# Queries of the second half of the tokens by Strassen's product, two tiles at a time, behind the keys and values

## The chip, the core and the metric

The kernel runs on one core of a Trainium2 chip. TensorE (PE) multiplies matrices into PSUM banks; VectorE (DVE), ScalarE (ACT) and GpSimd (POOL) work on what lies in PSUM and SBUF (POOL on SBUF alone here); SyncE (SP) and ACT issue the DMAs. The metric is the device time of one execution in microseconds (us), and the median of several executions where there are several.

## The reference: what is computed

The input x has 2048 tokens of 640 features. It is normalised per token (xn), and two branches work on xn:

```python
q, k, v = split(xn @ wqkv)                       # 32 heads of 20
phi(p) = concat(softmax(p @ w_phi), softmax(-p @ w_phi))   # 40 features a head, for q and for k
kv, z = phi_k^T v, sum of phi_k over the tokens  # per head
s = concat((phi_q kv) / (phi_q z + 1e-6)) @ wo   # linear attention
g = silu(gelu(xn @ w1 + b1) @ w2 + b2)           # feed-forward, 640 -> 1536 -> 640
out = x + s * g
```

All arrays are float32.

## The kernel before, in words

**Precision.** A float32 product is made of three passes (`PASSES`): each operand is rounded into a high part and the rest (`hi`, `lo`), and hi·hi, hi·lo and lo·hi are summed in PSUM. ACT makes the high part by a copy into a rounded type, DVE or POOL the rest by a subtraction.

**Folding.** The query and key weights are first multiplied by `w_phi` per head (`fold`, L166 to L173: 12 matmuls of 120 columns for each of five chunks of 128 input rows). `fold_w` (L176) rounds the result into one slab per chunk: `wk_s` and `wq_s`. The values' weights are `wv_s`.

**Stage 1, tiles of tokens.** 16 tiles of 128 tokens are taken in pairs: pair q holds tile 2q (even) and 2q+1 (odd); pairs 0 to 3 are the first half of the stage, 4 to 7 the second. `xp` (eight blocks of 128 rows, for four pairs) and the small slabs `b12` hold the rounded rows of a pair, `xd` (nine blocks) the rounded differences of blocks of the two tiles of a pair (`t_sums`, `t_split`, L274 to L282). Those differences exist for the feed-forward, which multiplies by Strassen's scheme in seven parts.

`project(t, ws)` (L321) multiplies one tile by one of the three weights: five chunks, three passes, two halves of 320 columns, so 30 matmuls of 128x320 into a slot of two PSUM banks (`bankA`, three slots in turn). Keys and queries then go through the features: `feat1` (L339) takes maximum, minimum, the difference to the maximum and `nr` = minimum - maximum on DVE, and the mirrored half on POOL (L351); `feat2` (L355) is one exponential on ACT. For keys, `key_fin` (L387) sums each head (DVE, L364), takes the reciprocal (L389) and scales on POOL (L369). `value` (L372) copies values out on ACT (L378). `query` (L381) stores the unnormalised exponentials to DRAM, from ACT's DMA queue. `kv_pair` (L404) adds two tiles to the running kv sum, 256 small matmuls into one bank of the `B` pool (two banks), which it keeps until `kv_rest` (L601) copies it out.

Tile t of the main loops (L517 and L546) does: keys of t, the preparation of a later pair of rows (statistics, mean subtraction L299 on POOL, product L304 on DVE, rounding L250 on ACT and L252 on DVE), values of t, features and scaling of the keys, and then queries: two at t = 6 to 9, one at t = 10 to 15, and two behind the loop. The folds of the query weights are spread over tiles 3, 4, 5 and 6.

**Stage 2, feed-forward and rest.** Twelve units (two halves of tokens by six groups of hidden columns): 54 matmuls of 128x512 in seven parts (`part`, L649 to L659), the activation, 60 matmuls back (`down`, L680 to L688). The weights of a group in Strassen's forms come from `w1_forms` (L411): sums on POOL (L414), rounding on ACT (L425) and POOL (L426). Then the normalised query features are transposed through DRAM, multiplied by kv (L790, L797) and by `wo` (L843).

**What sets the order.** All of stage 1 has its order written out by hand on every engine: each engine runs its instructions in the order of the program, and so does SP with its DMAs. A buffer is reused when its last reader is done; the pools matter here: `slabs` (23 of 5 KB per partition), `rows` (11), `bankA` (3 slots of two banks), `bankB` (2).

Of the kernel before, what the change touches and what calls it, by code (L numbers as in the profile page):

```python
# [8 lines left out]
F32 = mybir.dt.float32  # L9
# [6 lines left out]
P = 128  # L16
# [7 lines left out]
GF = 2  # L24
# [22 lines left out]
def hedgehog_gated_mlp_kernel(ctx: ExitStack, tc: tile.TileContext, x, xt_in, wqk, bd, wv, wo, w1, b1, w2, b2, out_t):  # L47
# [48 lines left out]
    xd_dram = dram.tile([P, 9, 2, CW], F32, name="xd_dram")  # L96
    w1_dram = dram.tile([NG, P, 2, 2048], F32, name="w1_dram")
    g_dram = dram.tile([KC, P, 2, CW], F32, name="g_dram")
    z_dram = dram.tile([1440], F32, name="z_dram")
    st_dram = dram.tile([NT // 2, 2, P, 2], F32, name="st_dram")  # L100

# [74 lines left out]
    def fold_w(tl, cs, name, dst):  # L176
# [6 lines left out]
            dst.append(sl)  # L183
        return mm, lo


    xts = {}
    last_feat, by_hand = [None], [True]
# [147 lines left out]
    def heads(ps):  # L336
        return ps[:, :, :HALF].rearrange("p a (h d) -> p a h d", d=DH)

    def feat1(ps):  # L339
# [3 lines left out]
        nc.vector.tensor_reduce(mx[:], p4, axis=AX.X, op=OP.max)  # L343
# [6 lines left out]
        last_feat[0] = nc.vector.tensor_tensor(nr[:], mn[:], mx[:], op=OP.subtract)  # L350
        nc.gpsimd.tensor_tensor(e5[:, :, :, 1, :], nr[:, :, :, None].to_broadcast([P, 2, 16, DH]),  # L351
                                e5[:, :, :, 0, :], op=OP.subtract)
        return e.rearrange("p a b -> p (a b)")

    def feat2(ef):  # L355
# [46 lines left out]
    vs, es, phis, xns, wk_s, wq_s = {}, {}, {}, {}, [], []  # L402

    def kv_pair(t):  # L404
        for u in (t, t + 1):
# [139 lines left out]
    queries = iter(range(NT))  # L545
    for t in range(6, NT):  # L546
        u = t + 4
        pk = project(t, wk_s)
        if u < NT:
            if u + 1 < NT:  # L550
                x_in(u + 1)
            if t > 6:
                pair_stats(u)
            if u % 2:
                load_xr(u // 2)
        if t in (6, 8):
            spill(t // 2 - 1)
        if t % 2 == 0 and 6 < t < NT - 2:
            pair_sub((t + 2) // 2)
        es[t] = feat1(pk)  # L560
        if t == 6:
            pair_stats(u)
            pair_sub(4)
            fold_w(wqT, range(4, KC), "wq", wq_s)
        if t % 2 == 0 and t < NT - 2:
            pair_mul((t + 2) // 2)
        if t == 12:
            w1r = load_w1(0)
        if t % 2 and t < NT - 2:
            t_sums((t + 1) // 2)  # L570
        vs[t] = value(t)
        feat2(es[t])
        phis[t] = key_fin(es.pop(t))
        if t % 2 == 0 and 6 < t < NT - 2:
            pair_plain((t + 2) // 2)
        if t % 2 and t < NT - 2:
            t_split((t + 1) // 2)
        if t == 6:
            query(next(queries))
            query(next(queries))  # L580
            pair_plain(4)
        if t == NT - 1:
            w1f = w1_forms(w1r)
            next(w1f)
            next(w1f)
        if t >= 7:
            query(next(queries))
        if t % 2 == 0:
            kv_pair(t - 2)
        if t == NT - 1:  # L590
            next(w1f)
        if 7 <= t < 10:
            query(next(queries))
    t = NT - 1
    w2r = [load_raw(w2[f * P:(f + 1) * P, :]) for f in range(GF)]
    pq = project(next(queries), wq_s)
    e_14 = feat1(pq)
    next(w1f)
    w1g = next(w1f)

    def kv_rest():  # L601
        kv_pair(NT - 2)
        kvr = const.tile([P, 424], F32, name="kvr")
        nc.scalar.activation(kvr[:, :320], kvp[0][:, :320], AF.Copy)
        nc.scalar.activation(kvr[:, 320:400], kvp[0][:, 240:320], AF.Copy)
        return kvr


    def kv_state(kvr):
        nc.gpsimd.memset(bdk[:, :, 60:], 0.0)  # L610
# [250 lines left out]
    def w2_raw(g):  # L861
        return [load_raw(w2[f * P:(f + 1) * P, :]) for f in range(g * GF, (g + 1) * GF)]

    kvr = kv_rest()
    e_last = feat1(project(next(queries), wq_s))
    startup.close()
    phase1.close()
    early_psum.close()
# [232 lines left out]
```

## Time and profile before

| | |
|---|---|
| runs shown | median 658.69 us (658.28 to 658.7, three) |
| profiled execution | 658.55 us, its span 656.8 us |
| granted clock of TensorE | 0.999 |
| instructions | 11378 |
| stage 1 on PE | 0.84 to 246.2 us of the span |
| feed-forward, first unit | from 246.23 us |

How to read it: the span runs from the first to the last instruction of the profiled execution. Rows of groups give the line, engine, operation, what it writes and reads, the shapes and the count, then busy us and mean ns of one, and the idle time before them with what ended it. Rows of the timeline and of the chain begin with the start and the length in us. L12 is line 12 of the kernel before. The ends of matmuls are modelled, so the distance between starts is the better measure for them.

### The profile page before, as it was taken

To read this page: it belongs to the slowest core of one execution; us is meant where nothing else is said; L and a number is where in the kernel's file an instruction comes from. 1 tells how busy PE (TensorE), PEld (TensorE's weight loads), DVE (VectorE), ACT (ScalarE), POOL (GpSimd) and SP (SyncE) were. 2 spreads that over 40 slices of the span, in tenths; PEclk is the share of its full clock that TensorE was granted. 3 is DMA by queue.
4 is the path that set the end of the run, shared out by engine and by line. 5 is a ranking of instruction groups with operands and counts; after the bars stand their busy time and mean duration, and the time that the engine had idled before them with its cause. 6 is when DMAs were issued, how large, how long until landed. Compare 5 with 4: busy or idle time off the path is not lost.

```text
span 656.8 us, 11378 instructions
## 1 busy us (share of the span) xinstructions
PE 651.7 (99%) x4438; PEld 567.1 (86%) x4438; DVE 472.9 (72%) x725; ACT 228.5 (35%) x320; POOL 381.3 (58%) x340
## 2 busy tenths in 40 slices
PE   9999999999999999999999999999999999999997
PEld 9999999999999998888888888888888886766866
DVE  5785865887878557678979968859889899853232
ACT  3523313423232227252352454752232424032130
POOL 2755354859577356958778876364462967343321
PEclk9999999999999999999999999999999999999999
DMA  9706052735261236436998899695769499999962
GB/s 350 275 1 173 7 158 91 248 82 156 51 219 51 102 94 254 135 126 234 246 250 305 198 410 327 100 335 215 153 225 231 95 268 206 307 215 252 283 222 81
DMA packets 159680, 126.97 MB, mean 193 GB/s; under 512 B 88978, under 2 KB 127122, under 8 KB 158730
## 3 DMA queue, kind: packets, MB, share of 16 engines
q1 hardware_dynamic: 156890, 114.64, 60.5%
q10 hardware_dynamic: 2736, 11.60, 4.7%
q8 instruction: 35, 0.57, 0.4%
q14 instruction: 19, 0.16, 0.1%
HBM read 81.12 MB, written 45.10 MB: 192 GB/s over the span
## 4 chain that ended last, share of the span: by engine, by line
PE 98%; DVE 1%; DMA 0%; SPq 0%; issue 0%; DVEq 0%
PE pA L330 32%; PE pB L688 24%; PE pB L659 22%; PE pB L843 11%; PE pA L171 2%; PE pB L790 2%; PE kv L398 2%; PE pA L462 1%; PE pB L797 1%; PE pA L316 1%; DVE y L697 0%; DMA phi_t<-eq 0%; DVE wolh L767 0%; DVE dn L364 0%; SPq L756 0%; DVE wol L768 0%
## 5 line engine op out<-in xcount | busy, mean ns | idle before, releaser
L688 PE MATMUL pB<-hs,w2s 128*128 128x512 f32 x720 | 165.8, 389 | 0.0
L688 PEld LDWEIGHTS pB<-hs,w2s 128*128 128x128 f32 x720 | 135.0, 188 | 28.8 <-DVE y L697 0.8
L659 PE MATMUL pB<-xp,w1s 128*128 128x512 f32 x324 | 81.4, 389 | 0.0
L659 PE MATMUL pB<-xd,w1s 128*128 128x512 f32 x324 | 79.3, 389 | 0.0
L356 ACT ACTIVATE e<-e 128x1280 f32<-128x1280 f32 x32 | 40.7, 1272 | 92.1 <-POOL e L351 91.7
L843 PE MATMUL pB<-oT,wo 128*128 128x512 f32 (+1 forms) x315 | 72.3, 381 | 0.0
L659 PEld LDWEIGHTS pB<-xp,w1s 128*128 128x128 f32 x324 | 60.7, 188 | 12.8 <-DVE pB L926 0.3
L659 PEld LDWEIGHTS pB<-xd,w1s 128*128 128x128 f32 x324 | 60.8, 188 | 12.6
L369 POOL TENSOR_TENSOR eq<-eq,rc 128x1280 f32<-128x1280 f32 x16 | 37.9, 2370 | 55.5 <-DVE rc L747 37.5
L843 PEld LDWEIGHTS pB<-oT,wo 128*128 128x128 f32 x315 | 57.2, 188 | 13.8 <-PE pB L790 2.5
L369 POOL TENSOR_TENSOR e<-e,rc 128x1280 f32<-128x1280 f32 x16 | 39.0, 2441 | 46.9 <-DVE rc L389 46.6
L697 DVE TENSOR_TENSOR y<-pB,y 128x512 f32<-128x512 f32 x100 | 63.1, 675 | 1.4 <-PE pB L688 1.4
L351 POOL TENSOR_TENSOR e<-nr,e 128x640 f32<-128x640 f32 x32 | 43.8, 1369 | 29.1 <-DVE nr L350 26.4
L330 PE MATMUL pA<-wv,xp 128*128 128x320 f32 x384 | 59.7, 310 | 0.0
L330 PE MATMUL pA<-wk,xp 128*128 128x320 f32 x384 | 59.7, 310 | 0.0
L664 ACT ACTIVATE pB<-pB,b1t 128x512 f32<-128x512 f32 x48 | 31.8, 662 | 78.7 <-DVE pB L926 29.3
L330 PE MATMUL pA<-wq,xp 128*128 128x320 f32 x384 | 58.8, 309 | 0.0
L330 PEld LDWEIGHTS pA<-wv,xp 128*128 128x128 f32 x384 | 57.0, 188 | 0.0
L330 PEld LDWEIGHTS pA<-wk,xp 128*128 128x128 f32 x384 | 56.9, 188 | 0.1
L330 PEld LDWEIGHTS pA<-wq,xp 128*128 128x128 f32 x384 | 56.9, 188 | 0.0
L734 POOL TENSOR_TENSOR ez<-eq,zrep 128x1280 f32<-128x1280 f32 x16 | 47.4, 2964 | 1.2 <-DVE y L695 1.2
L426 POOL TENSOR_TENSOR w1s<-raw,w1s 128x640 fp32r<-128x640 f32 (+1 forms) x18 | 26.3, 1462 | 30.0 <-ACT w1s L425 30.0
(137 smaller groups left out, 995.6 us busy)
## 6 DMA issues: line engine op xcount, KB each, us to landing
raw<-in_w_dram SPq DMA_DIRECT2D x42, 320.0 KB, 7.3
e_dram<-e ACTq DMA_DIRECT2D x16, 640.0 KB, 3.0
eq<-e_dram SPq DMA_DIRECT2D x16, 640.0 KB, 6.0
phi_t<-eq SPq DMA_DIRECT2D x64, 160.0 KB, 4.2
phT<-phi_t SPq DMA_DIRECT2D x20, 480.0 KB, 6.8
xres<-in_xt_dram SPq DMA_DIRECT2D x20, 256.0 KB, 4.6
xt<-in_x_dram SPq DMA_DIRECT2D x15, 320.0 KB, 5.3
out_dram<-xres SPq DMA_DIRECT2D x18, 256.0 KB, 8.5
```

The lines of the kernel that those rows point to most:

```text
L171: mm = nc.tensor.matmul(ps[:, hf, o:o + 120], tl[:120, c, i, :], foldb[:120, i, :120], start=True, stop=True)
L330: nc.tensor.matmul(ps[:, hf, :HALF], stat_x(q, o, k, a), ws[k][:, b, hf * HALF:(hf + 1) * HALF], start=n == 0, stop=n == 3 * KC - 1)
L351: nc.gpsimd.tensor_tensor(e5[:, :, :, 1, :], nr[:, :, :, None].to_broadcast([P, 2, 16, DH]), e5[:, :, :, 0, :], op=OP.subtract)
L356: nc.scalar.activation(ef, ef, AF.Exp)
L369: nc.gpsimd.tensor_tensor(e3, e3, rc[:, :, None].to_broadcast([P, 64, DH]), op=OP.mult)
L426: nc.gpsimd.tensor_tensor(sl[:, 1, :n], src, sl[:, 0, :n].bitcast(F32), op=OP.subtract)
L659: nc.tensor.matmul(bank[ch][:], tl[:, a, off + wo_:off + wo_ + P], mov(blk, b), start=new and n == 0, stop=n == len(mms) - 1, skip_group_c ...
L664: nc.scalar.activation(ps, ps, AF.Gelu_apprx_tanh, bias=b1t[:, f:f + 1])
L688: nc.tensor.matmul(ps[:], ws[i][:, b, d * P:(d + 1) * P], hs[o][i][:, a, :], start=i == n == 0, stop=(i, n) == (GF - 1, 2), skip_group_che ...
L697: nc.vector.tensor_tensor(y, ps[:], y, op=OP.add)
L734: nc.gpsimd.tensor_tensor(zv, ef, zf, op=OP.mult)
L843: nc.tensor.matmul(ps[:, mv], w, o[:, mv], start=n == 0, stop=n == 15, skip_group_check=True)
```

## The change

The second half's eight queries (pairs 4 to 7) leave the loop and come behind the last values, two tiles at a time, by the same seven parts that the feed-forward uses; the row blocks are the same (`xp`, `xd`), now as the stationary operand, and the weights are the halves and sums of the query weights.

- `fold_pair` (tiles 4 and 5) takes the place of four `fold_w` calls. Beside the rounded slabs it makes four sums of 128x320 from the two folded chunks, in two `sr` rows. `s_hi` rounds them on ACT, `s_lo` on POOL, and SP stores them to `s_dram`. At tile 15, `s_back` loads them into four slabs `wqs`.
- `query_pair` runs seven parts with 6, 6, 9, 9, 6, 9 and 9 matmuls of 128x320. X and W share the slot of the even tile, Z is in that of the odd tile, whose second bank DVE fills; Y and V take a bank of `B` each in turn. Copies of X and Y (ACT) and sums (POOL one, DVE four) stand between the parts.
- The statistics, x loads and splits (`t_split`) of later pairs are at other tiles; the first weight forms of the feed-forward, the exponential and scaling of tile 15 and the stores of the pairs are hooked between the parts; the POOL half of an odd tile's features comes in the next pair (`later`).
- The kv steps of tiles 12 to 15 and the copy of the kv bank come behind the first and the second pair.

The diff, cut to its core:

```diff
+    def fold_pair(i):
+        pa, pb = (fold(wqT, c)[0] for c in (i, 2 + i))
+        a, b = (row([P, D], F32, "sr") for _ in range(2))
+        for c, ps in ((i, pa), (2 + i, pb)):
+            wq_s[c] = slab(F32R, f"wq{c}")
+            s3 = wq_s[c][:].rearrange("p s (a b) -> p s a b", a=2)
+            nc.scalar.activation(s3[:, 0], ps[:, :, :HALF], AF.Copy)
+            nc.vector.tensor_tensor(s3[:, 1], ps[:, :, :HALF], s3[:, 0].bitcast(F32), op=OP.subtract)
+        dve = lambda d, x, y, op: nc.vector.tensor_tensor(d, x, y, op=op)
+        nc.scalar.activation(b[:, HALF:], pa[:, 1, :HALF], AF.Copy)
+        dve(a[:, HALF:], pa[:, 0, :HALF], b[:, HALF:], OP.subtract)
+        dve(b[:, HALF:], pb[:, 1, :HALF], b[:, HALF:], OP.add)
+        dve(a[:, :HALF], b[:, HALF:], pa[:, 0, :HALF], OP.subtract)
+        dve(b[:, :HALF], pb[:, 0, :HALF], a[:, :HALF], OP.subtract)
+        return [(i, a), (2 + i, b)]
...
+    def s_lo(parts):
+        for k, r, hi in parts:
+            nc.gpsimd.tensor_tensor(r[:].bitcast(F32R), r[:], hi[:].bitcast(F32), op=OP.subtract)
+            nc.sync.dma_start(s_dram[k][:, 0], hi[:].bitcast(F32))
+            nc.sync.dma_start(s_dram[k][:, 1], r[:])
...
@@ tiles 2 to 5
-        if t == 5:
-            fold_w(wqT, range(2, 3), "wq", wq_s)
...
+        if t >= 4:
+            if t == 5:
+                s_lo(s_hi(srs[0]))
+            srs.append(fold_pair(t - 4))
         feat2(es[t])
         if t == 4:
             pair_plain(3)
-        if t >= 3:
-            fold_w(wqT, range(t - 3 + (t > 4), t - 2 + (t > 4)), "wq", wq_s)
         phis[t] = key_fin(es.pop(t))
+        if t == 5:
+            s_lo(s_hi(srs[1]))
...
+    QPARTS = (("X", "A11", 0, None), ("Y", "S2", 10, None), ("X", "A12", 2, ("A1k", 4)), ("V", "S3", 12, ("A2k", 7)),
+              ("Z", "S1", 8, None), ("W", "A22", 14, ("A2k", 16)), ("Z", "S4", 5, ("A1k", 7)))
...
+    def query_pair(q, hooks, later):
+        even, odd = bankA(), None
+        bank, seen = {"X": even[:, 0, :HALF], "W": even[:, 1, :HALF]}, set()
+        r1 = row([P, 2, HALF], F32, "qx")
+        r2 = row([P, 2, HALF], F32, "qu")
+        for i, (ch, wn, xb, extra) in enumerate(QPARTS):
+            if ch in "YV":
+                bank[ch] = bankB("q" + ch)[:, :HALF]
+            if i == 4:
+                odd = bankA()
+                bank["Z"] = odd[:, 0, :HALF]
+            mms = [(wn, k, b, xb + k, a) for k in range(2) for a, b in PASSES]
+            if extra:
+                mms += [(extra[0], 0, b, extra[1], a) for a, b in PASSES]
+            for n, (w, k, b, blk, a) in enumerate(mms):
+                nc.tensor.matmul(bank[ch], q_x(blk, a, q), q_weight(w, k)[:, b], start=ch not in seen and n == 0,
+                                 stop=n == len(mms) - 1, skip_group_check=True)
+            seen.add(ch)
+            if i == 0:
+                nc.scalar.activation(r1[:, 0], bank["X"], AF.Copy)
+            elif i == 1:
+                nc.scalar.activation(r1[:, 1], bank["Y"], AF.Copy)
+                nc.gpsimd.tensor_tensor(r2[:, 0], r1[:, 0], r1[:, 1], op=OP.add)
+            elif i == 3:
+                nc.vector.tensor_tensor(r2[:, 1], r2[:, 0], bank["V"], op=OP.add)
+            elif i == 4:
+                nc.vector.tensor_tensor(odd[:, 1, :HALF], r2[:, 1], bank["Z"], op=OP.add)
+            elif i == 5:
+                nc.vector.tensor_tensor(bank["W"], r2[:, 1], bank["W"], op=OP.add)
+                ee = feat1(even)
+            elif i == 6:
+                nc.vector.tensor_tensor(bank["Z"], r2[:, 0], bank["Z"], op=OP.add)
+            if i in hooks:
+                hooks[i]()
+        return ee, feat1(odd, later)
...
@@ tiles 6 to 15
+    XIN = {6: (11, 12), 7: (13, 14), 8: (15,)}
+    STATS = {7: (11,), 8: (12, 13), 9: (14, 15)}
+    XR = {7: 5, 9: 6, 11: 7}
...
-        if t == 12:
+        if t == 13:
             w1r = load_w1(0)
-        if t % 2 and t < NT - 2:
+        if t in (7, 9, 11, 13):
             t_sums((t + 1) // 2)
+        if t == NT - 1:
+            s_back()
+        if t == NT - 1:
+            t_split(7)
         vs[t] = value(t)
...
+        if t in (7, 9):
+            t_split((t + 1) // 2)
+        if t == 12:
+            t_split(6)
...
-        if t >= 7:
-            query(next(queries))
-        if t % 2 == 0:
-            kv_pair(t - 2)
...
+        if t % 2 == 0 and t < NT - 2:
+            kv_pair(t - 2)
         if 7 <= t < 10:
             query(next(queries))
...
+    for q in range(4, 8):
+        if q == 7:
+            w2r = [load_raw(w2[f * P:(f + 1) * P, :]) for f in range(GF)]
+        ea, eb = query_pair(q, {1: lambda: early_rest(q, ea), 3: lambda: late_rest(q, eb), **({0: lambda: feat2(es[NT - 1])} if q == 4 else {})}, later)
+        if q == 4:
+            kv_pair(NT - 4)
+        if q == 5:
+            kv_pair(NT - 2)
+            kvr = kv_rest()
```

`early_rest` (behind part Y) and `late_rest` (behind V) issue, for the pair before, the POOL half of its odd tile, its exponentials and its stores, and one step of `w1_forms`; in the first pair `early_rest` scales tile 15's keys.

More of the change, by code (lines that the diff above doesn't have):

```diff
@@ L184, in fold_w, with s_hi @@
         return mm, lo
+    srs = []
+    def fold_pair(i):
[13 more added lines that the diff above has]
+        return [(i, a), (2 + i, b)]
+    def s_hi(pairs):
+        out = []
+        for k, r in pairs:
+            hi = row([P, D], F32R, "sh")
+            nc.scalar.activation(hi[:], r[:], AF.Copy)
+            out.append((k, r, hi))
+        return out
+    def s_lo(parts):
[3 more added lines that the diff above has]
+            nc.sync.dma_start(s_dram[k][:, 1], r[:])
     xts = {}
@@ new lines, in store_e, with kv_rest @@
+    def store_e(t, ef):
+        nc.scalar.dma_start(e_dram[_tok(t)], feat2(ef))
+    def kv_rest():
+        kvr = const.tile([P, 424], F32, name="kvr")
+        nc.scalar.activation(kvr[:, :320], kvp[0][:, :320], AF.Copy)
+        nc.scalar.activation(kvr[:, 320:400], kvp[0][:, 240:320], AF.Copy)
+        return kvr
+    wq_f = []
+    queries = iter(range(NT // 2))
+    XIN = {6: (11, 12), 7: (13, 14), 8: (15,)}
+    STATS = {7: (11,), 8: (12, 13), 9: (14, 15)}
+    XR = {7: 5, 9: 6, 11: 7}
@@ L576, in hedgehog_gated_mlp_kernel @@
[L576 to L577 removed]
+        if t in (6, 8, 10, 12):
+            pair_mul(q)
+        if t == 13:
+            w1r = load_w1(0)
+        if t in (7, 9, 11, 13):
+            t_sums((t + 1) // 2)
+        if t == NT - 1:
+            s_back()
+        if t == NT - 1:
+            t_split(7)
+        vs[t] = value(t)
+        if t < NT - 1:
+            feat2(es[t])
+            phis[t] = key_fin(es.pop(t))
+        if t in (8, 10, 12):
+            pair_plain(q)
```

95 lines of the change are left out of this document (50 added, 45 removed).

## The prediction

> **What bounds the kernel now.** First the page: busy shares, granted clock, and the chain that ended last.
>
> ```profile
> span 656.8 us, 11378 instructions
> PE 651.7 (99%) x4438; PEld 567.1 (86%) x4438; DVE 472.9 (72%) x725; ACT 228.5 (35%) x320; POOL 381.3 (58%) x340
> PEclk9999999999999999999999999999999999999999
> PE 98%; DVE 1%; DMA 0%; SPq 0%; issue 0%; DVEq 0%
> ```
>
> TensorE (PE) is busy for 651.7 of 656.8 us at full clock, and 98% of the chain is PE's own work. So the next question is whether PE ever waits: the view of waits for PE, then the window of the stage that the change rebuilds.
>
> ```profile
> PE pA L462 <- PEq L1091: 0.8, 1, 0.8
> PE pB L797 <- DVE y L697: 0.4, 1, 0.4
> 158.00:246.00 88.00, 88.00 (x1073) 87.02 (x1072) 59.36 (x76) 25.82 (x30) 54.00 (x50) 1.00 0.34 107
> ```
>
> Two waits, 1.2 us in all, none in the projections. The window's columns are length, then PE, PEld, DVE, ACT and POOL: from 158 to 246 us PE has no gap, DVE is busy for 59 us and POOL for 54. So each matmul taken out here is worth its spacing, as long as the engines that empty the banks keep up. The spacing stands in the chain in order of time:
>
> ```profile
> 53.00 1.33 PE pA L171 x12
> 54.33 8.80 PE pA L330 x60
> 63.13 1.33 PE pA L171 x12
> ...
> 272.29 12.24 PE pB L659 x54
> ```
>
> Sixty matmuls of 320 columns take 8.80 us, **146.7 ns** each; the 54 of 512 columns of a feed-forward unit take 12.24 us, 226.7 ns. The last row matters twice: those 54 are the same seven parts that the change gives the queries, six or nine matmuls in a row into one bank. The two spacings differ by 80.0 ns for 192 columns, 0.417 ns a column, and both leave 13.3 ns beside the columns. Going by parts costs no more per matmul than going by projections.
>
> **What leaves PE.** Two tiles of queries cost 2 x 30 = 60 matmuls. A pair by parts costs 6+6+9+9+6+9+9 = 54, all still 128x320: 54 x 146.7 ns = 7.92 us in place of 8.80. Four pairs save 24 x 146.7 ns = **3.52 us**. Five folds of 12 matmuls, keys, values, the first eight queries and eight kv steps keep their number and only move.
>
> **What is added beside PE.** The prices, by line and shape in the stage from 80 to 247 us, and single rows of the timeline:
>
> ```profile
> L350 DVE TENSOR_TENSOR nr<-mn,mx 128x32 f32<-128x32 f32 x25 | 14.5, 579 | 0.0
> L351 POOL TENSOR_TENSOR e<-nr,e 128x640 f32<-128x640 f32 x24 | 33.0, 1378 | 25.2 <-DVE nr L350 23.0 <-issue 1.9
> L356 ACT ACTIVATE e<-e 128x1280 f32<-128x1280 f32 x24 | 30.6, 1273 | 87.5 <-POOL e L351 87.1 <-ACT e L356 0.4
> L369 POOL TENSOR_TENSOR e<-e,rc 128x1280 f32<-128x1280 f32 x11 | 27.2, 2473 | 26.7 <-DVE rc L389 26.3
> L364 DVE TENSOR_REDUCE rc<-e 128x64 f32<-128x1280 f32 x11 | 16.3, 1484 | 23.4 <-ACT e L356 23.4
> L389 DVE RECIPROCAL rc<-rc 128x64 f32<-128x64 f32 x11 | 6.1, 553 | 0.4
> L282 POOL TENSOR_TENSOR xd<-tt,xd 128x1152 fp32r<-128x1152 f32 x4 | 10.8, 2692 | 0.0
> L414 POOL TENSOR_TENSOR st<-raw 128x256 f32<-128x256 f32 x2 | 1.5, 741 | 0.0
> L426 POOL TENSOR_TENSOR w1s<-raw,w1s 128x640 fp32r<-128x640 f32 x1 | 1.6, 1567 | 0.0
> ```
>
> ```profile
> 52.08 0.42 DVE L252 TENSOR_TENSOR b<-pA,b 128x256 fp32r<-128x256 f32 x1 [0.54 <-ACT xp L250]
> 52.42 0.55 DVE L252 TENSOR_TENSOR xp<-pA,xp 128x384 fp32r<-128x384 f32 x1
> 55.53 0.82 DVE L182 TENSOR_TENSOR wq<-pA,wq 128x640 fp32r<-128x640 f32 x1 [2.57 <-ACT wq L181]
> 66.10 1.49 DVE L304 TENSOR_TENSOR xr<-xr,bc 128x1280 f32<-128x1280 f32 x1 [3.56 <-POOL xr L299]
> 208.06 0.82 DVE L343 TENSOR_REDUCE mx<-pA 128x32 f32<-128x640 f32 x1 [0.38 <-PE pA L330]
> ...
> 210.26 2.62 DVE L350 TENSOR_TENSOR nr<-mn,mx 128x32 f32<-128x32 f32 x1
> ```
>
> *Folds (tiles 4 and 5).* Each `fold_pair` adds four DVE sums of 320 columns from PSUM: between the 0.42 us for 256 columns and the 0.55 for 384, so 0.48, about 0.40 from start to start. They hold two of the three bankA slots longer, and the next value takes the first of them. With one fold fewer before it, tile 4 starts at 53.0, its folds end at 64.5, and value 5 asks for the slot at 70.2. DVE's product ends near 66.3 (now 67.6, a fold later); two roundings and three sums behind it end near 69.0. In tile 5 the second fold asks at 75.9 for the slot of key 5, which DVE leaves near 75.1 (from 69.4: rounding 1.5, sums 1.5, reciprocal 0.5, features 2.2). **Cover about 1 us each time, cost nothing**; if DVE comes later, PE waits by the excess, once per tile. ACT's copies, POOL's four subtractions (1.57 us each) and the eight stores on SP stand ahead of x rows, statistics and feature halves that are wanted a tile later: nothing.
>
> *Keys and values alone (tiles 10 to 15).* The window of 88 us holds the eight queries that go to the pairs: 35.2 us of PE, 8 x 1.38 of POOL and 8 x 2.7 of DVE. What stays has 52.8 us of PE for at most 43 us of POOL and 38 of DVE: nothing, though any pair of x rows that comes late stops PE by what it is late.
>
> *Weights back.* Four loads of 640 KB on SP, ahead of the last value:
>
> ```profile
> e_dram<-e ACTq DMA_DIRECT2D x16, 640.0 KB, 3.0
> eq<-e_dram SPq DMA_DIRECT2D x16, 640.0 KB, 6.0
> ```
>
> Their slabs come free, at the latest, as the last key projection uses up its weights, every 0.88 us. From its start, S2 is wanted after 9.7 us and S1 after 13.2. At 6.0 us each, overlapping: nothing; one after the other at 3.0 to 6.0, up to about 2 us once.
>
> *The query pairs.* At 0.88 us for six matmuls and 1.32 for nine, X ends at 0.88, Y 1.76, A12 3.08, V 4.40, Z 5.28, W 6.60, Z again at 7.92. New waits stand in PE's only queue, and the whole rest stands behind them. How long an emptied bank takes:
>
> ```profile
> 246.91 0.41 ACT L604 ACTIVATE kvr<-kv 128x320 f32<-128x320 f32 x1
> 247.65 0.60 ACT L675 ACTIVATE x<-pB 128x512 f32<-128x512 f32 x1 [0.20 <-PE pB L659]
> ```
>
> A12 waits for X's copy: 0.20 to start and 0.41 to run, 0.61 of the 0.88 us that Y gives. V needs the one B bank that kv leaves, so Y's copy: 0.61 of 1.32. The last part waits for DVE's sum of Z: 0.20 + 0.48 of W's 1.32. All fit if the engine is free. Once it isn't: in the first pair ACT has the exponential of tile 15 (1.27 us) between the copies. X's copy ends at 1.49, the exponential at 2.77, Y's copy at 3.2, and V starts at 3.25, not 3.08: **+0.17 us**. POOL's sum there stands behind a split (2.69) and tile 15's second half, which leaves the last part some 0.6 us of room. For all other waits, 0 to 1.5 us, I take 0.2: the rows leave room nearly everywhere.
>
> *Moved besides.* The kv steps of the last four tiles now follow the first and second pair, and the two copies of the kv bank follow them on ACT, ahead of the third pair's X copy: kv ends 0.88 us before X does, which covers 0.41 and a short second copy. The stores of exponentials go out from ACT in the pairs: two copies, two exponentials and one rounding, near 4 us of 7.92. On SP the loads of w1 go a tile later and those of w2 stay ahead of the feed-forward by at least a pair: nothing. Tile 15's scaling on POOL (2.47) is wanted only after the second pair.
>
> DVE does per pair two feature groups (2.20 from the maximum's start to that of `nr`, and 0.51 for `nr`) and four sums: 2 x 2.71 + 4 x 0.40 = **7.0 of 7.92 us**. It ends the last pair some 4.5 us behind PE. The feed-forward begins on the slot freed longest ago and comes to the last one as its fifth bank: nothing. Its first weight forms now come ahead of it.
>
> **The sum.** 658.55 (the profiled execution, 1.75 above its span) - 3.52 + 0.17 + 0.2 = 655.4 us. The median of the runs shown, 658.69, lies 0.14 above that execution: **655.5 us**.
>
> **Rivals.** *Small waits eat half.* Copies and POOL's sums come late in every pair. At 0.4 us a pair, 655.5 + 1.6 = 657.1. For it: POOL has up to 29 us of work in these 34 us (second halves 8 x 1.38, sums near 4 x 0.9, forms 4 x 0.74 + at most 4 x 1.57, a scaling and a split 5.2). Against: most of it is wanted a pair later.
>
> *DVE becomes the bound, and the kernel slower.* `nr` can stand behind POOL:
>
> ```profile
> 210.15 2.69 POOL L282 TENSOR_TENSOR xd<-tt,xd 128x1152 fp32r<-128x1152 f32 x1
> ...
> L350 DVE TENSOR_TENSOR nr<-mn,mx x32: 172/265/2624, 21.5 to 248.5; 128x32 f32<-128x32 f32 x32
> ```
>
> The `nr` at 210.26 took 2.62 us and ended as POOL's split did; the shortest took 0.17. POOL is fuller in the pairs than it was beside the queries. If every `nr` waits out a whole rounding of 1.57 us, a pair takes 2 x (2.2 + 1.7) + 1.6 = 9.4 us of DVE, 1.5 over PE: 655.2 + 4 x 1.5 = 661.2; at 2.6 each, 668. It decides from a mean `nr` of 1.4 us, where a pair takes 8.8. Against: the median is 0.265, most of POOL's operations here last 0.7 to 1.6 us, and the added sums read one operand from PSUM. The Trainium skill (SBUF — State Buffer, "Who interferes with whom") says that a VectorE instruction with two SBUF inputs and a GpSimd one that reads SBUF take one shared port in turn, each for its whole length, and that one SBUF input does not contend. By that rule `nr` is the only feature step exposed and the four sums are not; the 2.62 us row agrees.
>
> *No saving per matmul.* Were a matmul by parts to take 163 ns, 54 would cost the old 8.80: 658.7. The feed-forward's 226.7 ns speak against it.
>
> **Chances.** Forecast 0.66 (654.9 to 656.3 by itself), small waits 0.14, DVE bound 0.13, no saving 0.07. About 0.2% (1.3 us) is what a measurement of this kernel can tell from no change, so faster means below 657.4: 0.66 + 0.10 = 0.76; same 0.04 + 0.05 = 0.09; slower 0.13 + 0.02 = 0.15. Forecast and small waits hold 0.80: from 654.6 (nothing waits, less run to run spread) to 658.2 (1.5 us of waits in pairs, 1 at the folds and weights).
>
> **What will show it.** 1440 matmuls of 128x320 become 1416. The pairs should take 7.92 us each on PE, with a wait near 0.17 us before V of the first; the view of waits for PE should list little else in pA and pB. DVE should be near 7 us busy per pair, with `nr` near 0.6 us. Wrong would be a PE idle over 0.5 us in every pair (small waits), DVE without idle from the second pair on (DVE bound), waits on pA at 70 or 76 us (folds), a wait on the load of S2 or S1, or a spacing other than 146.7 ns.

## The result and the profile after

The change takes 661.31 us (median of 5 runs, 660.64 to 661.65) against 658.69 for the kernel before (5 runs, 658.2 to 658.89): ratio **1.0041**, interval 1.0026 to 1.0055. It is slower by 2.6 us; the prediction was 655.5, and its range ended at 658.2. First the head of the page and the shares of the chain, the same rows that were shown of the kernel before:

```profile
span 659.6 us, 11407 instructions
PE 649.7 (99%) x4414; PEld 564.1 (86%) x4414; DVE 486.5 (74%) x749; ACT 235.0 (36%) x334; POOL 390.5 (59%) x348
PE 67%; DVE 8%; POOL 3%; ACT 1%; issue 1%; DMA 0%; DVEq 0%; POOLq 0%
```

PE has its 24 matmuls fewer (4414 records for 4438) and 2.0 us less to do, and still the span is 2.8 us longer. PE's share of busy time, 99%, tells nothing of it. The chain does: PE fell from 98 to 67%, because the way back from the end now leaves PE in stage 1: from 217.04 us, where V of the first pair starts, back to 158.75 us it runs through DVE, POOL and ACT without one matmul. The view of PE's waits says where (in all, times, longest):

```profile
PE pA L363 <- DVE nr L383: 2.1, 2, 1.8
PE qV L616 <- ACT qx L622: 1.6, 1, 1.6
PE kv L435 <- issue: 0.9, 1, 0.9
PE pA L499 <- PEq L1211: 0.8, 1, 0.8
PE pB L919 <- DVE y L819: 0.4, 1, 0.4
```

The last two (the sequencer's L1211 and the feed-forward's `y`) stood before as well. The first three are new, and the timeline of PE places them (start, length, and in brackets the wait):

```profile
128.47 0.83 PE L435 MATMUL kv<-e,v 128*32 128x40 f32 x67
130.19 1.47 PE L435 MATMUL kv<-e,v 128*32 128x40 f32 x61 [0.88 <-issue]
131.59 2.02 PE L363 MATMUL pA<-wq,b 128*128 128x320 f32 x12
...
140.88 1.99 PE L363 MATMUL pA<-wv,b 128*128 128x320 f32 x12 [0.23 <-DVE nr L383]
...
198.91 4.64 PE L363 MATMUL pA<-wv,xp 128*128 128x320 f32 x30 [1.83 <-DVE nr L383]
...
217.04 1.14 PE L616 MATMUL qV<-wqs,xd 128*128 128x320 f32 x6 [1.61 <-ACT qx L622]
...
231.51 1.40 PE L435 MATMUL kv<-e,v 128*32 128x40 f32 x128
232.84 1.43 PE L616 MATMUL pA<-wq,xp 128*128 128x320 f32 x6
234.10 1.04 PE L616 MATMUL qY<-wqs,xd 128*128 128x320 f32 x6
...
249.06 1.55 PE L781 MATMUL pB<-xp,w1s 128*128 128x512 f32 x6
```

Starts are the better measure. The kv step of tiles 6 and 7 takes 131.59 - 128.47 = 3.12 us where the one at 231.51 takes 1.33: 1.8 lost, of which the view calls 0.88 a wait. Value 9 comes 0.4 late, value 14 2.0 (196.91 was due, by 146.7 ns a matmul), V of the first pair 1.8 (due at 213.95 + 1.32), and X of the third pair takes 1.26 for 0.88: 0.4. That is 6.4 us. The feed-forward began at 246.06 before (start of its first row; the kernel before):

```profile
246.06 1.55 PE L659 MATMUL pB<-xp,w1s 128*128 128x512 f32 x6
```

It begins 3.0 us later now, and 3.0 + 3.52 saved = 6.5: the losses account for the result. Behind that point the two kernels run alike: 610.5 us of span are left for 610.7 before.

**Two places, one chain.** The two large waits, at value 14 and at V, lie on the same way back. For value 14, DVE's part of the timeline of the kernel after, then POOL's:

```profile
191.01 2.58 DVE L285 TENSOR_TENSOR b<-xr,b 128x256 fp32r<-128x256 f32 x1
193.52 3.05 DVE L285 TENSOR_TENSOR xp<-xr,xp 128x384 fp32r<-128x384 f32 x1
...
198.69 0.18 DVE L383 TENSOR_TENSOR nr<-mn,mx 128x32 f32<-128x32 f32 x1
```

```profile
190.56 2.75 POOL L406 TENSOR_TENSOR e<-e,rc 128x1280 f32<-128x1280 f32 x1 [3.44 <-DVE rc L426]
193.28 2.87 POOL L315 TENSOR_TENSOR xd<-tt,xd 128x1152 fp32r<-128x1152 f32 x1
...
214.09 1.28 POOL L384 TENSOR_TENSOR e<-nr,e 128x640 f32<-128x640 f32 x1 [0.19 <-DVE nr L383]
```

DVE's two roundings of 256 and 384 columns take 2.58 and 3.05 us; the prediction's rows for these shapes, with one operand in PSUM, have 0.42 and 0.55. Here both operands lie in SBUF, and each ends within 0.5 us of POOL's instruction beside it: DVE at 193.59 and 196.57, POOL at 190.56 + 2.75 = 193.31 and 193.28 + 2.87 = 196.15. The features of tile 13 start behind them (196.49), and value 14 waits for their bank. The Trainium skill (SBUF — State Buffer, "Who interferes with whom") says that a VectorE instruction with two SBUF inputs contends with a GpSimd one that reads SBUF; the trace agrees.

Only the second of the two is new. The same roundings in the kernel before:

```profile
195.24 2.58 DVE L252 TENSOR_TENSOR b<-xr,b 128x256 fp32r<-128x256 f32 x1
197.74 0.55 DVE L252 TENSOR_TENSOR xp<-xr,xp 128x384 fp32r<-128x384 f32 x1
```

There too the first stood beside POOL's scaling (194.79 to 197.54), but POOL then had nothing to do: pair 6 had been split in tile 11 (183.09). The change moved this split to tile 12, beside the second rounding, and that is 2.5 us more for DVE.

For V, the row of ACT that matters:

```profile
215.40 1.27 ACT L393 ACTIVATE e<-e 128x1280 f32<-128x1280 f32 x1 [1.69 <-POOL e L384]
216.57 0.42 ACT L622 ACTIVATE qx<-qY 128x320 f32<-128x320 f32 x1
```

The exponential of tile 15 stands ahead of Y's copy, as foreseen, but it starts at 215.40, when POOL's second half (214.09) is done, and not when X's copy is.

### The profile page after: what moved, and what is told of

Its sections match the earlier page's. It is cut to its first block, busy times and chain, and to the rows that moved or that the text cites. A ratio compares the mean times of both kernels' runs of the same rounds, so it can differ in the third digit from the quotient of the medians.

```text
span 659.6 us, 11407 instructions
## 1 busy us (share of the span) xinstructions
PE 649.7 (99%) x4414; PEld 564.1 (86%) x4414; DVE 486.5 (74%) x749; ACT 235.0 (36%) x334; POOL 390.5 (59%) x348
## 4 chain that ended last, share of the span: by engine, by line
PE 67%; DVE 8%; POOL 3%; ACT 1%; issue 1%; DMA 0%; DVEq 0%; POOLq 0%
PE pB L810 24%; PE pB L781 22%; PE pB L965 11%; PE pA L616 3%; PE pA L363 3%; PE pB L912 2%; POOL e L384 2%; DVE b L285 1%; DVE rc L401 1%; ACT e L393 1%; DVE xp L285 1%; DVE nr L383 1%; PE qV L616 1%; DVE mx L376 1%; DVE mn L377 1%
## 5 line engine op out<-in xcount | busy, mean ns | idle before, releaser
L401 DVE TENSOR_REDUCE rc<-e 128x64 f32<-128x1280 f32 x16 | 23.7, 1483 | 23.5 <-ACT e L393 23.5
L968 POOL TENSOR_TENSOR xres<-gt,xres 128x256 f32<-128x256 f32 x20 | 14.3, 736 | 35.7 <-DVE gt L967 35.7
```

The costliest lines, as they stand in the source:

```text
L401: nc.vector.tensor_reduce(ss[:], ef.rearrange("p (g d) -> p g d", d=DH), axis=AX.X, op=OP.add)
```

## The experiments

Theory A: the matmuls saved are really saved, and the loss is order: work of DVE, POOL and ACT stands too late in their queues, above all in tiles 10 to 15 and the first pair, where the query projections that gave these engines 4.4 us a tile are gone. Theory C: the gap in the kv step comes from the two big stores beside it, which hold up PE's instructions. The rivals stand in the expectations: a chain too long in whatever order, or parts whose copies and sums eat the saving. All the matmuls stay in every kernel unless an edit says so. Line numbers shift by some lines from kernel to kernel.

### One wait or one suspect at a time

*e1: tile 15's exponential behind Y's copy.*

```diff
-{1: ..., 3: ..., **({0: lambda: feat2(es[NT - 1])} if q == 4 else {})}
+{1: ..., 3: ...}      # feat2(es[NT - 1]) first in early_rest, hook 1
```

> The changed kernel, but tile 15's exponential stands behind the copy of Y instead of ahead of it. Theory A (the key features come late on DVE and POOL in tiles 8 to 15, and the first pair inherits it through that exponential): V's wait of 1.8 us in the first pair falls under 0.3 us, the time from 661.3 to about 659.6 us; the other waits stay. Rival B (the parts themselves wait, for the one B bank or for the weights loaded back): V still waits 1 us or more, 661 us.

Measured: 661.07 us (660.45 to 661.59), ratio 1.004 [1.0025, 1.0055]. V's wait is gone, and no time is won. Value 14 waits 1.83 us as before, and this time TensorE ran slower behind the wait; PE's row, and two windows (length, busy PE, PEld, DVE, ACT, POOL, then the granted clock, the share of the DMA engines and GB/s):

```profile
199.28 6.17 PE L363 MATMUL pA<-wv,xp 128*128 128x320 f32 x30 [1.83 <-DVE nr L383]
```

```profile
200.00:202.00 2.00, 2.00 (x12) 2.00 (x11) 0.01 (x1) 1.27 (x1) 2.00 (x4) 0.70 0.00 0
202.00:204.00 2.00, 2.00 (x9) 2.00 (x8) 1.97 (x3) 0.00 (x0) 1.92 (x6) 0.50 0.00 0
```

Thirty matmuls take 6.17 us for 4.64: 1.5 us of the 1.8 that V no longer lost. That is the profiled run (661.59 us, mean clock 0.996). The three others had 0.999 and 1.000, too high for such a drop, and took 660.45 to 661.11; what kept them from the 659.6 expected is not shown.

*e2: POOL's split of pair 6 at tile 14.*

```diff
-        if t == 12:
+        if t == 14:
             t_split(6)
```

> The changed kernel, but POOL's split of pair 6 stands at tile 14 instead of tile 12. Theory A, in its form with the shared port (DVE's last rounding of pair 7 took 3.05 us because POOL's split ran, and the features of tile 13 came late): that rounding takes 0.55 us, value 14 no longer waits (2.0 us now), 658.8 to 659.3 us. Rival D (DVE has too much to do there whatever POOL does): the wait of value 14 falls by less than 0.7 us, 660.7 us or more.

Measured: 662.62 us (662.24 to 664.1), 1.0068 [1.0051, 1.0085]. The rounding of 384 columns is back at 0.55 us while that of 256 keeps its 2.59, and the wait at value 14 is gone: its cause is shown. V then waits twice as long, to the same moment (217.15 for 217.04). DVE's row, then PE's:

```profile
194.02 0.55 DVE L285 TENSOR_TENSOR xp<-xr,xp 128x384 fp32r<-128x384 f32 x1
```

```profile
217.15 1.15 PE L616 MATMUL qV<-wqs,xd 128*128 128x320 f32 x6 [3.29 <-ACT qx L622]
```

PE came to the pair 1.6 us earlier and DVE to the `nr` of tile 15 2.0, but the exponential of tile 15 did not: POOL now did the moved split (211.56, 2.67 us) ahead of tile 15's second half (214.20). Behind the wait the granted clock fell to 0.54 and 0.61 from 218 to 222 us, and the feed-forward begins 1.4 us later than in the change (250.42).

*e3: projections in place of the parts, in the change's order.*

```diff
-        ea, eb = query_pair(q, ...
+        ea, eb = query_two(q, ...     # project(2 * q), feat1, project(2 * q + 1), feat1
```

> The changed kernel with everything in its place, but the eight queries behind the values go by ordinary projections, 60 matmuls per pair; the sums of weights are still made and loaded and nobody uses them. Theory A (the loss comes from the order, the gain of the parts is there): 24 matmuls more cost 3.5 us, V's wait of 1.8 is gone, so about 663.1 us, with the wait of value 14 still near 2 us. Rival B (the parts cost what they save): 661.3 us or less.

Measured: 663.12 us (662.4 to 664.26), 1.0073 [1.0058, 1.0088], value 14 waits 1.82. So going by parts was worth 1.8 us in the change as it stands, and the order, together with the sums of weights that nobody uses here, costs 4.7 (663.12 - 658.46, the kernel before beside it).

*e4: the stores of exponentials 2 and 3 at tile 4.*

```diff
-        nc.scalar.dma_start(e_dram[_tok(t)], ef)
+        # t in (2, 3): kept, and both issued behind the store of t == 4
```

> The changed kernel, but the two stores of the exponentials of tiles 2 and 3, which ran just ahead of the kv step of tiles 6 and 7, are issued some 18 us later. Theory C (in that kv step PE ran out of instructions, because their fetch stood behind those stores): the gap of some 1.8 us in the step goes, 659.5 us. Rival (the gap has to do with where the step lies in PE's program, or is chance): it stays at the same place, 661.3 us, or is absent in the other kernels of this call too.

Measured: 663.09 us (661.88 to 663.78), 1.0069 [1.0054, 1.0084]. PE's rows:

```profile
128.88 1.39 PE L442 MATMUL kv<-e,v 128*32 128x40 f32 x128
...
141.32 1.88 PE L363 MATMUL pA<-wv,b 128*128 128x320 f32 x7 [2.05 <-DVE e L380]
```

The stores are the cause: the kv step (128 matmuls in the trace, not the 256 of the description of the kernel) has no gap. Whether they held up instructions, the second half of theory C, is another question (last section). But no time is won, since value 9 now waits 2.05 us for DVE and starts at 141.32 for 140.88. In tiles 6 to 9 too DVE sets when PE goes on, and the gap only hid it. Behind the wait the clock fell (0.50 from 142 to 144 us): the value's 30 matmuls take 147.35 - 141.32 = 6.0 us for 4.4, which makes e4 slower than the change.

### Two moves, and the cause in tiles 6 to 9

*e5: e1 and e2 together.*

> The exponential of tile 15 stands behind the copy of Y, and POOL's split of pair 6 comes at tile 14 instead of 12: both moves at once, each of which alone left one of the two waits standing. If the wait at value 14 (1.83 us) and the one before V of the first pair (1.61 to 1.77 us) come from one late chain of DVE and POOL in tiles 10 to 15 that can be put off (theory A): both below 0.3 us, 3.6 us less than 661.3, so 657.7. If that chain is too long whatever its order (rival): one of the two places, or the last part of the first pair, still waits over 1 us, 659.5 or more.

Measured: 661.36 us (659.63 to 663.19), 1.0042 [1.0027, 1.0057]. Theory A's number failed: both waits are gone, but the last part of the first pair waits 2.82 us. PE's row, then DVE's:

```profile
219.96 1.38 PE L616 MATMUL pA<-wqs,xp 128*128 128x320 f32 x6 [2.82 <-DVE pA L627]
```

```profile
216.56 1.49 DVE L401 TENSOR_REDUCE rc<-e 128x64 f32<-128x1280 f32 x1 [5.18 <-ACT e L393]
...
219.41 0.50 DVE L627 TENSOR_TENSOR pA<-qu,pA 128x320 f32<-128x320 f32 x1
```

DVE sat idle 5.18 us for tile 15's exponential, with the key sums of tile 15 ahead of the sums of V and Z in its queue; POOL's sum of Y stood behind two splits. That is wrong order again, or a chain that is too long; this run can't tell the two apart.

*e6: e4, and the statistics of tiles 7 to 9 behind that tile's maxima. e7: e4, and the rounding and stores of the second pair of S sums behind tile 6's features.*

```diff
-        for u in STATS.get(t, ()):
-            pair_stats(u)
         ...
             pair_mul(q)
+        for u in STATS.get(t, ()):      # e6
+            pair_stats(u)
```

```diff
-        if t == 5:
-            s_lo(s_hi(srs[1]))
         ...
             fold_w(wqT, range(4, KC), "wq", wq_s)      # t == 6
+            s_lo(s_hi(srs[1]))                         # e7
```

> The stores of exponentials 2 and 3 leave at tile 4 (as in the run before, which took 663.1 us and had a wait of 2.05 us at value 9), and the statistics of tiles 7 to 9 stand behind that tile's maxima and products, so that DVE does them while it would wait for the exponential. If the two statistics in one tile are the main cause of DVE's lateness at value 9: its wait falls to 0.75 us or less, the drop of the clock behind it goes, and the time is 660 to 661.5. If the cause is the rounding of the S sums and the full pool of rows at tile 6 (rival): the wait stays at 1.3 us or more, 662 to 663.

> The stores of exponentials 2 and 3 leave at tile 4, and the rounding of the second pair of S sums, with its four stores, stands behind the features of tile 6 instead of at the end of tile 5. If the S sums and the full pool of rows make DVE late from tile 6 on: the wait at value 9 falls from 2.05 us to 0.3 or less, 660 to 661. If the two statistics in one tile are the cause (rival): the wait stays at 1 us or more, 662 to 663.

Measured: e6 663.21 us (662.74 to 664.06), 1.0072 [1.0057, 1.0087]; e7 668.08 (667.65 to 669.88), 1.015 [1.0135, 1.0165]. Value 9 waits 0.79 us in e6 and not at all in e7, so both causes count, the S sums more. DVE's product for pair 4, in the kernel before, the change and e7:

```profile
92.72 1.49 DVE L304 TENSOR_TENSOR xr<-xr,bc 128x1280 f32<-128x1280 f32 x1 [2.82 <-POOL xr L299]
```

```profile
94.92 1.49 DVE L337 TENSOR_TENSOR xr<-xr,bc 128x1280 f32<-128x1280 f32 x1 [4.95 <-POOL xr L332]
```

```profile
91.65 2.82 DVE L337 TENSOR_TENSOR xr<-xr,bc 128x1280 f32<-128x1280 f32 x1 [2.83 <-POOL xr L332]
```

The S sums held POOL, and pair 4's rows came 2.2 us later. Both totals missed: PE came earlier to the later tiles and waited longer there (a kv step 1.49 and 1.37 us for POOL's scaling, V 3.44 and 3.64 us), and e7 has a new wait ahead of the feed-forward:

```profile
254.55 2.93 PE L787 MATMUL pB<-xp,w1s 128*128 128x512 f32 x6 [4.41 <-DVE e L380]
```

Its releaser, DVE's last product at 253.69, belongs to the odd tile of pair 7, the last that DVE empties; the change has no such wait. The reading is that the edit turned the rotation of the three slots, so that the feed-forward's first bank is another one; no trace shows a bank's number, and e9 and e11 test it.

*e8: all five moves (e1, e2, e4, e6, e7).*

> All five moves at once: stores of exponentials 2 and 3 at tile 4, statistics behind the maxima, rounding of the second pair of S sums behind tile 6's features, the split of pair 6 at tile 14, the exponential of tile 15 behind the copy of Y. The matmuls are those of the change. If the loss is all order (theory A for tiles 10 to 15, theory C and DVE's lateness for tiles 6 to 9): no wait over 0.5 us in stage 1, the feed-forward starts near 243, and the time is 655 to 656.5, below the kernel before. If DVE and POOL have too much to do in these stages whatever the order (rival): waits of 1 us or more are left in pA or qV, 658 or more.

Measured: 661.23 us (660.57 to 662.16), 1.0043 [1.0028, 1.0057]: missed. From 84 to 213 us PE loses 0.2 us in all. Then the last part of the first pair waits 2.12 us, as in e5, with a clock of 0.50 behind it (219 to 221 us), and the feed-forward waits 1.68, on a bank of pair 7's even tile.

### The first pair

*e9: e8, with tile 15's key sums (DVE) and the split of pair 7 (ACT and POOL) behind the sum of Z, and a DVE memset of one column in tile 13 that turns the slots by one. e10: the first pair's moves on e5. e11: e9 without the memset. e12: e9 with projections.*

```diff
+        if t == 13:                                          # not in e10, e11
+            nc.vector.memset(bankA()[:, 0, :1], 0.0)
-        if t == NT - 1:
-            t_split(7)
         ...
+    def behind_z():                                          # hook 4 of the first pair
+        phis[NT - 1] = key_fin(es.pop(NT - 1))
+        t_split(7)
+        w1g.append(next(w1f))
```

> The run with all five moves (661.2 us) still lost time at two places: 2.12 us before the last part of the first pair, behind which the clock fell, and 1.68 us before the feed-forward, whose first bank was the one of pair 7's even tile. Here, on top of the five moves, the key sums of tile 15 on DVE and the split of pair 7 stand behind the sum of Z in the first pair, and one VectorE memset of one column in tile 13 turns the three slots of bankA by one, so that the feed-forward's first bank is one that is free early. If the loss is all order (theory A): no wait over 0.5 us in stage 1, the feed-forward starts near 243.5, 661.2 - 2.1 - 1.7 - about 1.2 for the clock = 655.4 to 656.6. If DVE and POOL have too much to do whatever the order (rival): a wait of 1 us or more appears in a later pair or earlier tile, 657.5 or more.

> The change with the moves of tiles 12 to 15 and the first pair alone: exponential of tile 15 behind the copy of Y, split of pair 6 at tile 14, key sums of tile 15 and split of pair 7 behind the sum of Z. Stores, statistics and S sums stand as in the change. If the wait of 2.82 us before the last part came from DVE's sums standing ahead of the two of V and Z: it is gone, with the drop of the clock behind it, and 661.4 - 2.8 - 1.2 to 1.5 = 657.0 to 657.5; the gap of about 1 us in the kv step of tiles 6 and 7 stays. If putting it off only moves the wait (rival): a wait of 1 us or more in the first or second pair, 659 or more.

> The first kernel of this job without the memset of one column: the feed-forward's first bank is again that of pair 7's even tile. If the bank sets the wait before the feed-forward: 1.5 to 2 us there, ended by DVE's nr of that tile, and that much more time, 657.1 to 658.5. If not (rival): no wait, the same time as the first kernel.

> The first kernel of this job with the last eight queries as projections (30 matmuls a tile) in the place of the parts, in the same order: it costs 24 matmuls more on TensorE. If the parts bring their 146.7 ns a matmul once nothing waits: 3.5 us more than the first kernel, about 659.5. If the parts' copies and sums take back a share (rival): 2.5 us or less more, or the first kernel shows waits that are gone here.

Measured: e9 661.93 us (661.26 to 662.9), 1.0055 [1.0043, 1.0068]; e10 662.73 (662.38 to 663.72), 1.0069 [1.0056, 1.0083]; e11 662.87 (661.65 to 664.73), 1.0072 [1.0056, 1.0087]; e12 660.3 (659.43 to 660.88), 1.0028 [1.0016, 1.004]. Here the rivals were right. The first pair of e9 has no wait; the second stops PE for 3.04 us. PE, DVE and POOL of e9:

```profile
228.76 1.97 PE L621 MATMUL pA<-wqs,xp 128*128 128x320 f32 x6 [3.04 <-DVE pA L632]
```

```profile
220.10 2.57 DVE L383 TENSOR_TENSOR nr<-mn,mx 128x32 f32<-128x32 f32 x1
...
227.62 0.49 DVE L630 TENSOR_TENSOR qu<-qu,qV 128x320 f32<-128x320 f32 x1 [2.04 <-POOL qu L628]
```

```profile
217.62 2.37 POOL L406 TENSOR_TENSOR e<-e,rc 128x1280 f32<-128x1280 f32 x1 [4.08 <-DVE rc L433]
219.94 2.68 POOL L315 TENSOR_TENSOR xd<-tt,xd 128x1152 fp32r<-128x1152 f32 x1
...
226.72 0.87 POOL L628 TENSOR_TENSOR qu<-qx 128x320 f32<-128x320 f32 x1
```

`nr` of 32 columns takes 2.57 us, to the end of POOL's split (222.62): the rival's mechanism, in one place. But it is not what stops PE, for DVE then sits idle 2.04 us until POOL's sum of Y is done (227.59). POOL had waited 4.08 us for DVE's reciprocal, with the scaling, the split, four sums and the sum of Y behind it in its queue. e10 has the same wait at the same place (3.5 us). The parts were then no gain: e12, with 24 matmuls more, is 1.6 us faster than e9. The memset of tile 13 cost 1.3 us itself (its slot is emptied by DVE, and key 14 waits for it). e11's wait ahead of the feed-forward (1.7 us on pair 7's even tile, none in e9) confirms that turning the slots decides it; its time does so only roughly.

### The splits early

*e13: e8, with both splits where POOL idles. e14: e13 with projections. e15: e13 without the moves of tiles 4 to 9 (e4, e6, e7). e16: e13 with tile 15's key sums behind the sum of Z.* In e13 the split of pair 6 stands ahead of tile 14's exponential; ACT's half of pair 7's comes at the end of tile 14, POOL's half behind tile 15's second half of features; one memset takes the first bank of the feed-forward, so that its first part gets another.

```diff
         vs[t] = value(t)
+        if t == 14:
+            t_split(6)
         if t < NT - 1:
             feat2(es[t])
         ...
         if t == 14:
-            t_split(6)
+            t_hi(7)
         ...
         if t == NT - 1:
-            t_split(7)
+            t_split(7, False)      # POOL's half alone
         ...
+        if unit == 0:
+            nc.vector.memset(bankB()[:, :1], 0.0)
```

> The five moves, and the splits early: the split of pair 6 stands ahead of tile 14's exponential, the ACT half of pair 7's split at the end of tile 14 and its POOL half behind tile 15's second half of features, so that GpSimd does both where it waited for DVE's reciprocals. One memset on DVE takes the feed-forward's first bank, so that its first part gets a bank that is free early. If the loss is all order (theory A): POOL ends tile 15's second half near 210.2 in place of 212.7, the exponential ends near 212.3, the sums of V and Z come 0.3 us late at most, no wait over 0.5 us in the pairs, the feed-forward starts near 243.6, and 661.2 - 2.1 - 1.7 - 1.3 + 0.3 = 656.4 (655.6 to 657). If the parts leave DVE and POOL no room (rival): a wait of 1 us or more in the first or second pair, 658.5 or more.

> The first kernel of this job with the last eight queries as projections (30 matmuls a tile) in place of the parts, in the same order: 24 matmuls more, but none of the parts' copies and sums. If the parts bring their 146.7 ns a matmul once the order is right (theory A): 3.5 us more than the first kernel, about 659.9. If the parts' copies and sums take it back (rival): the same time as the first kernel or less.

> The change with the moves of tiles 12 to 15 alone, as in the first kernel of this job: stores, statistics and S sums of tiles 4 to 9 stand as in the change, so the kv step of tiles 6 and 7 keeps its gap of about 1 us and value 9 its wait of up to 0.4 us. If most of the loss is in tiles 12 to 15 and the first pair (theory A): 1.0 to 1.5 us more than the first kernel, about 657.6. If both stages matter as much (rival): 2.5 us more or above, 659 or more.

> The first kernel of this job with DVE's key sums of tile 15 (1.49 + 0.55 us) behind the sums of V and Z instead of ahead of them. If these sums are all that holds the first pair (theory A): 0.3 us less than the first kernel, 656.1. If the second pair then meets DVE late, as it did once (3.04 us there, behind a nr that waited 2.57 us for a split; rival): 1 us or more above the first kernel.

Measured: **e13 656.68 us** (7 runs, 655.17 to 657.24), ratio **0.997** [0.996, 0.9981], faster than the kernel before (658.4 beside it) and 4.6 us faster than the change; e14 658.98 (657.82 to 659.84), 1.0008 [0.9998, 1.0017]; e15 658.24 (657.96 to 658.96), 0.9998 [0.9989, 1.0007]; e16 656.89 (655.93 to 657.35), 0.9974 [0.9964, 0.9985]. The profile of e13: head, PE's waits, its first row of the feed-forward, and POOL's rows:

```profile
span 653.5 us, 11405 instructions
PE 648.3 (99%) x4414; PEld 563.5 (86%) x4414; DVE 485.2 (74%) x750; ACT 235.4 (36%) x334; POOL 390.7 (60%) x348
```

```profile
PE pA L510 <- PEq L1226: 0.8, 1, 0.8
PE pB L932 <- DVE y L832: 0.4, 1, 0.4
```

```profile
242.95 1.55 PE L794 MATMUL pB<-xp,w1s 128*128 128x512 f32 x6
```

```profile
202.50 2.70 POOL L319 TENSOR_TENSOR xd<-tt,xd 128x1152 fp32r<-128x1152 f32 x1
...
208.54 1.28 POOL L388 TENSOR_TENSOR e<-nr,e 128x640 f32<-128x640 f32 x1 [0.19 <-DVE nr L387]
209.77 2.69 POOL L319 TENSOR_TENSOR xd<-tt,xd 128x1152 fp32r<-128x1152 f32 x1
```

POOL's second half for tile 15 starts at 208.54, 0.9 us after the first pair began (1.9 in the change), and only the two waits of the kernel before are left. DVE's key sums and the sums of V and Z still come a little late: the first pair's last part begins at 214.60 where 214.29 was due, and up to there the chain followed back has no matmul from 125 us on. So the other engines set the pace up to that point in e13 too; it costs only 0.3 us there. The busy times are those of the change (POOL 390.7 for 390.5, DVE 485.2 for 486.5): the same work, another order. The feed-forward starts 3.1 us ahead of the kernel before, of 3.52 saved.

e15 misses its 657.6 by 0.6, but it is clearly nearer to theory A: the moves of tiles 12 to 15 are worth 661.31 - 658.24 = 3.1 us, those of tiles 4 to 9 another 1.6. e14 says what the parts bring in a good order: 2.3 us by the medians (3.0 between the two profiled runs, 3.2 between their feed-forwards, 246.15 and 242.95), less than the 3.5 expected and not nothing. e16 decides nothing: 0.2 us from e13, inside its spread. Why single runs of e13 lie between 655.2 and 657.2, with no wait in the profiled one (655.32), stays open.

## Why the prediction was wrong

- **24 x 146.7 ns = 3.52 us: right.** The parts keep the spacing. PE's rows of the fourth pair, six matmuls in 0.88 us and nine in 1.32:

```profile
242.02 1.04 PE L616 MATMUL qY<-wqs,xd 128*128 128x320 f32 x6
242.90 1.48 PE L616 MATMUL pA<-wq,xp 128*128 128x320 f32 x9
244.22 1.04 PE L616 MATMUL qV<-wqs,xd 128*128 128x320 f32 x6
```

- **"Keys and values alone: nothing": the step that failed.** It set 52.8 us of PE against sums of 43 and 38 us of POOL and DVE. These engines do not work side by side: a key goes DVE, POOL, ACT, DVE, POOL, and each waits for the last. In the change this chain runs from 158.75 to 217.04 us without a matmul in it. Beside this the step took DVE's 38 us from the kernel before, where one of the two roundings was stretched by POOL (2.58 and 0.55 us); the split that the change moved stretched the other as well (3.05), 2.5 us more in one tile. Before, 4.4 us of query projection in each tile covered such lateness. The step named the mechanism ("any pair of x rows that comes late stops PE by what it is late") and gave it no price: 2.0 us at value 14, and the lateness that V then waits for.
- **"+0.17" for V of the first pair: the right wait, but it measured 1.8 us.** It was worked out as if tile 15's features were done when the pair began. The pair began at 212.19; POOL came to the second half of these features 1.9 us later and ACT to the exponential 3.2 us later, with the copy of Y behind it in ACT's queue.
- **Folds: right for the waits it looked for** (no wait on pA from 53 to 84 us), **wrong for what it called wanted "a tile later: nothing".** The S sums' rounding came ahead of pair 4's rows on POOL, as the step says, and that was not nothing: 2.2 us of lateness that DVE carried to tile 9. With two statistics in one tile it ended in PE's wait there.
- **0.2 us for other waits, bounds 0 to 1.5: too narrow.** The kv step's gap of 1.8 us was not among the kinds of wait considered: PE stood beside two stores, with no engine to wait for (below).
- **Weights back, DVE in the pairs: right.** No wait on the loads of S. The eight `nr` of the pairs take 0.58 us on average (longest 1.58), where near 0.6 was forecast, and no part of a pair waits for DVE. The rival "DVE becomes the bound" did not make this change slow by way of `nr`; the sharing that it rests on did, at a rounding where the prediction did not look.
- **"The feed-forward begins on the slot freed longest ago": true of the change, which has no wait there, by the luck of the rotation:** e7 and e8 wait 4.4 and 1.7 us.
- **The range** reached 658.2 by adding small waits inside the pairs and at the folds and weights. It had no case for lateness in tiles 6 to 15, where the change takes matmuls away and leaves the other engines' work.

## What to carry to other kernels

Matmuls taken out of a stage are also cover taken from the other engines there: follow one tile's chain through all of its engines, queue by queue, against the new distance between PE's instructions, and never set busy sums against each other. When one wait is removed and the next appears with the end unmoved, the chain behind both is the bound; what helped here was to move work into the idle time that an engine spends waiting ahead of it (POOL's 3.4 us before its scalings), not to push it back. Check by name which bank or slot the next stage begins on, since any edit can turn the rotation.

## What the runs showed that was not expected

- **A wait can cost twice.** In e1 a wait of 1.83 us was followed by a granted clock of 0.50 to 0.70 for about 4 us (1.5 us lost); in the change the same wait at the same place was followed by 1.00. In e9, behind 3.04 us, it was 0.50 from 230 to 232 us. In the profiled runs, all ten waits of PE of 2.05 us and more (e2, e4 to e11) were followed within six us by 2 us at 0.54 or less, and of eleven waits of 1.28 to 1.83 us only that of e1 was. So a reordering that leaves one wait of 2 us pays for it again, which is part of why e2, e4, e5 and e8 missed. The Trainium skill (TensorE: Matmul & The Clock Gate, "What's actually happening") ties the lower clock to an idle window of about 3.4 us that runs freely. That the drop came behind one wait and not behind its twin fits a window that runs freely; that 1.83 and 2.05 us were enough does not fit its length.
- **A kv step can stand still beside bulk stores.** In the change two stores of 640 KB left at 124.94 and 126.61 us. The DMA engines were full until 129 us and busy at 0.50 and 0.36 in the two us after it, when PE stood (129.3 to 130.2 us) and then went on slowly; with the stores moved (e4) the same 128 matmuls ran through in 1.33 us. That the stores cause the gap is shown: the profiles of the kernels that leave them in place (e1 to e3, e5, e10, e15) have one of 0.6 to 1.2 us there, those that move them have none. That they held up PE's instructions is not: the trace's instruction queues moved nothing from 128.2 to 131.6 us, while only the stores' queue was at work. What PE lacked stays open.
